# Four blocks of attention and gated MLP: order of the first V pass, of block 1's score sums, and of their store and reload against the weight loads

## The chip, the core and the metric

The kernel runs on one core of one Trainium2 chip. The metric is the device time of one execution in microseconds (us). Executions of the kernel before differ by up to about 1.8 us (1617.65 to 1619.47 us), so effects under 0.5 us are read from the traces, not from the times.

Engine names in the profile: PE is TensorE, PEld its weight load, DVE is VectorE, ACT is ScalarE, POOL is GpSimd, SPq is the queue of SyncE, which issues nearly all DMAs of this kernel in one fixed order.

## The reference, cut to what matters

```python
x = A_x                                            # 2048 tokens x 1024, bf16
x = x + _A_ref(_layernorm(x), A_wqkv, A_wo)        # local dilated attention: 32 heads of 32, 8 keys, step 2
x = x + _B_ref(_layernorm(x), W_gate, W_up, W_down)  # relu(gate) * up, 3584 hidden
x = x + _A_ref(_layernorm(x), A_wqkv, A_wo)
x = x + _B_ref(_layernorm(x), W_gate, W_up, W_down)
```

## The kernel before

Tokens go in blocks of 512 (four tiles of 128). While PE does the gate/up matmuls of block 0, VectorE does the attention of block 1. All steps are "events" with a planned time; sorting the events by that time gives each engine's order of instructions. The planned times set only this order: an instruction runs when its engine reaches it and its data are there. `GRP` (1.73) is the planned time of eight 128x512 matmuls; `t_gu0`, called `at` in the loop, is the planned start of block 0's gate/up matmuls.

The head, the first 11 us (shortened): LayerNorm of block 0, transposed on PE, then V products that start with tile 0 alone.

```python
    def turn(t, halves=(0, 1)):                 # eight transposes; tile 1's in two calls of four
        if t in tps: pass
        elif t == 0: tps[t] = [psum.tile(... tag="acc") for h in range(2)]         # two PSUM tiles
        else:                                                                      # one pair tile
            both = psum_l.tile([P, 2, KC, P], BF16, tag="L", name="tp_pair"); ...
    act_square(2); act_mean(2)                  # ScalarE: tile 2's sums, ahead of the copies
    ...; turn(0); copy(0, "a", ...) x2; ...     # ScalarE copies tile 0's transposes
    def head():
        for kc in range(KC // 2):
            if kc == KC // 2 - 1: ln["second"](0)      # tile 1: first half of the turn, its copy
            for c in range(KC): prod(kc, c, 0, 1)      # V products of tile 0
        ln["second"](1)                                # tile 1: second half
```

Block 1's score sums: sixteen VectorE steps (a product of q and k, an addition), stored to DRAM in two halves, reloaded in another layout, then added over the partitions (`u<-s` in the profile), softmax, weighted V sums (`pv`).

```python
    spread(sums1[:4], t_pv0 + 34.5, 4.5)
    spread(sums1[4:6], t_wo0 + 0.5, 2.5)
    spread(sums1[6:10], t_fill + 1.4, 4.6)
    spread(sums1[10:], t_gu0 + 2.6, 5.4)
    ...
            ev.append((at + 37.5, store_s(1, 1)))        # second half of the sums to DRAM, 0.5 MB
            ev.append((at + 40.5, load_s(1)))            # reload, 4 DMAs, 1 MB in all
            spread(gets2, at + 36.0, 2.5)                # q and k of block 2
            spread(softmax_steps(1), at + 52.0, 3.6)     # starts with u<-s, which waits for the reload
            spread(pv_steps(1), at + 63.0, 5.3)
```

The weights come as 1 MB slabs through a ring of five buffers. A slab load is an event 0.3 after the planned end of the slab whose buffer it takes; an up slab and a gate slab stand at `at + 24 * GRP + 0.3`, that is `at + 41.82`, behind store and reload.

## Time and profile before

| | before |
|---|---|
| time, median of 6 runs | 1618.11 us (1617.65 to 1619.47) |
| span of the profiled run | 1616.4 us |
| PE busy | 1611.3 us |
| PE waits | 1.5 and 0.4 us, both before 9 us |

Two parts of the page of the kernel before: PE's busy time, and the chain of work that ended last.

```profile
PE 1611.3 (100%) x7633; PEld 786.6 (49%) x7633; DVE 1137.1 (70%) x960; ACT 475.8 (29%) x968; POOL 180.4 (11%) x168
PE 99%; DMA 0%; ACT 0%; DVE 0%; issue 0%; ACTq 0%; DVEq 0%
```

The waits of PE in the kernel before (what waited, for whom: us in total, times, longest):

```profile
PE scratch L132 <- DVE ones L310: 1.5, 1, 1.5
PE acc_v L132 <- ACT xnT_first L328: 0.4, 1, 0.4
```

PE is the bound everywhere, and past 9 us it waits for nobody. A change can win only in the head, and can lose anywhere by making a new wait.

The timeline of PE in the head of the kernel before (start and duration in us, engine, line, operation, names, shapes, count, idle before it and what ended it; the last line of each such view is cut off by the end of its window, so its count says nothing):

```profile
6.97 0.72 PE L385 MATMUL tp<-ident,xn_first 128*128 128x128 bf16 x8
8.09 1.50 PE L132 MATMUL acc_v<-xnT_first,w_v 128*128 128x128 bf16 x24 [0.40 <-ACT xnT_first L328]
9.51 0.40 PE L385 MATMUL tp_pair<-ident,xn_first 128*128 128x128 bf16 x4
9.74 0.61 PE L132 MATMUL acc_v<-xnT_first,w_v 128*128 128x128 bf16 x8
10.42 0.38 PE L385 MATMUL tp_pair<-ident,xn_first 128*128 128x128 bf16 x4
10.64 0.55 PE L132 MATMUL acc_v<-xnT_first,w_v 128*128 128x128 bf16 x7
```

The first V product comes 1.12 us after tile 0's first transpose, tile 1's first product (10.64) 3.67 us after it.

The DMA queue of the kernel before around the second store of the sums (same columns; a line is an issue, and its duration is the time to issue, not the transfer):

```profile
230.70 0.34 SPq L121 DMA_DIRECT2D s_d<-s  x1
231.09 0.42 SPq L121 DMA_DIRECT2D k<-k_d  x1
233.90 4.38 SPq L121 DMA_DIRECT2D s<-s_d  x4
238.32 1.46 SPq L121 DMA_DIRECT2D q<-q_d  x1
239.88 0.39 SPq L121 DMA_DIRECT2D w_u<-in_B_W_up_dram  x1
240.32 1.31 SPq L121 DMA_DIRECT2D w_g<-in_B_W_gate_dram  x1
```

The up slab landed at 246.9 and its first matmul started at 247.27: a margin of 0.4 us.

`hT` are the gate products, the VectorE instructions that free PE's accumulators.

### The profile page before, as it was taken

The page shows a single profiled execution, that of the slowest core. Times are in us where ns is not written, and L with a number is a line of the kernel's source. Part 1 is how long each engine was busy: PE and PEld are TensorE (multiplying, and loading weights), DVE is VectorE, ACT ScalarE, POOL GpSimd, SP SyncE. Part 2 cuts the span into 40 slices and gives each one's busy share as a digit, 9 for nine tenths or more (in the row PEclk, how much of TensorE's full clock was granted, in tenths as well). Part 3 has the DMA queues.
Part 4 walks back from the last instruction along what each step waited for, and adds up shares of the span by engine and source line. Part 5 has one row for each costly group of instructions (what it writes and reads, how often), then busy time and mean ns, then how long its engine had stood idle before and what let it go on. Part 6 is the DMA issues. An engine that isn't in the chain of part 4 may idle for free.

```text
span 1616.4 us, 18930 instructions
## 1 busy us (share of the span) xinstructions
PE 1611.3 (100%) x7633; PEld 786.6 (49%) x7633; DVE 1137.1 (70%) x960; ACT 475.8 (29%) x968; POOL 180.4 (11%) x168
## 2 busy tenths in 40 slices
PE   9999999999999999999999999999999999999999
PEld 6646544444444445444454444544445444444444
DVE  5999989996989698929489293893939939311211
ACT  5853312132116313603136031361313311131110
POOL 2400100010003002300053000530005100000000
PEclk9999999999999999999999999999999999999999
DMA  9868868697669766794847947479574794755452
GB/s 306 180 190 238 224 159 262 183 216 204 208 192 217 200 184 212 192 246 146 227 160 201 240 153 230 152 205 252 165 226 155 203 245 157 209 161 177 157 167 68
DMA packets 407448, 317.92 MB, mean 197 GB/s; under 512 B 166464, under 2 KB 387008, under 8 KB 406848
## 3 DMA queue, kind: packets, MB, share of 16 engines
q1 hardware_dynamic: 406784, 316.13, 69.9%
q8 instruction: 59, 0.97, 0.3%
q10 hardware_dynamic: 576, 0.59, 0.1%
q14 instruction: 29, 0.24, 0.0%
HBM read 266.29 MB, written 34.66 MB: 186 GB/s over the span
## 4 chain that ended last, share of the span: by engine, by line
PE 99%; DMA 0%; ACT 0%; DVE 0%; issue 0%; ACTq 0%; DVEq 0%
PE acc_u L132 24%; PE acc_g L132 24%; PE dacc L132 18%; PE acc_v L132 7%; PE acc_wo L132 7%; PE acc_k L132 7%; PE acc_q L132 7%; PE dacc_pair L132 6%; DMA x<-in_A_x_dram 0%; ACT xn_first L328 0%; PE tp_pair L385 0%; PE L L132 0%; DVE x L837 0%; DVE xnT_first L106 0%; ACTq L175 0%
## 5 line engine op out<-in xcount | busy, mean ns | idle before, releaser
L132 PE MATMUL acc_g<-xnT_b,w_g 128*128 128x512 bf16 x1792 | 423.3, 379 | 0.0
L132 PE MATMUL acc_u<-xnT_b,w_u 128*128 128x512 bf16 x1792 | 423.3, 379 | 0.0
L790 ACT ACTIVATE r<-acc_g 128x512 bf16<-128x512 f32 x224 | 133.5, 596 | 726.7 <-PE acc_g L132 701.6
L106 DVE TENSOR_TENSOR hT<-acc_u,r 128x512 bf16<-128x512 f32 x224 | 150.5, 685 | 240.7 <-PE acc_u L132 238.2
L132 PE MATMUL dacc<-w_d,hT 128*128 128x512 bf16 (+1 forms) x1400 | 301.9, 375 | 0.0
L132 PEld LDWEIGHTS <-hT 128*128 128x128 bf16 x1820 | 178.1, 98 | 208.9
L132 PEld LDWEIGHTS <-w_u 128*128 128x128 bf16 x1792 | 175.3, 98 | 211.5
L132 PEld LDWEIGHTS <-w_g 128*128 128x128 bf16 x1792 | 175.4, 98 | 211.4
L106 DVE TENSOR_TENSOR pv<-a,vhm 128x4096 bf16<-128x4096 bf16 x64 | 143.4, 2281 | 0.0
L837 DVE TENSOR_TENSOR x<-dacc,x 128x512 bf16<-128x512 f32 (+1 forms) x38 | 24.5, 672 | 154.2 <-PE dacc L132 154.2
L608 DVE TENSOR_TENSOR t<-q,k 128x2048 f32<-128x2048 bf16 x56 | 128.0, 2292 | 6.7 <-ACT k L543 4.6
L106 DVE TENSOR_TENSOR t<-q,k 128x2048 f32<-128x2048 bf16 x56 | 127.4, 2285 | 3.7 <-ACT k L543 2.6
L106 DVE TENSOR_TENSOR pv<-pv 128x1024 bf16<-128x1024 bf16 (+1 forms) x128 | 113.6, 947 | 0.0
L549 POOL COPY kh<-k 128x14 bf16<-128x14 bf16 x40 | 56.0, 1406 | 504.3 <-ACT k L543 504.3
L132 PE MATMUL acc_wo<-w_o,oT 128*128 128x512 bf16 x512 | 111.8, 379 | 0.0
L621 DVE TENSOR_TENSOR ac<-ac,t 128x2048 f32<-128x2048 f32 x48 | 109.6, 2284 | 0.3
L106 DVE TENSOR_TENSOR ac<-ac,t 128x2048 f32<-128x2048 f32 x48 | 109.5, 2282 | 0.0
L264 POOL TENSOR_TENSOR st_b<-st_b,neg_half 128x1 f32<-128x1 f32 x29 | 43.9, 1523 | 525.8 <-ACT st_b L263 525.7
L132 PE MATMUL dacc_pair<-w_d,hT 128*128 128x512 bf16 x420 | 95.9, 379 | 0.0
L132 PEld LDWEIGHTS <-oT 128*128 128x128 bf16 x512 | 50.0, 98 | 60.4
L259 ACT ACTIVATE xn_b<-x 128x1024 bf16<-128x1024 bf16 x29 | 30.3, 1045 | 129.1 <-DVE x L106 67.0
L446 ACT CAST vT<-acc_v 128x512 bf16<-128x512 f32 x56 | 32.8, 588 | 57.6 <-PE acc_v L132 56.6
(134 smaller groups left out, 1230.0 us busy)
## 6 DMA issues: line engine op xcount, KB each, us to landing
w_g<-in_B_W_gate_dram SPq DMA_DIRECT2D x56, 1024.0 KB, 7.4
w_u<-in_B_W_up_dram SPq DMA_DIRECT2D x56, 1024.0 KB, 5.5
w_d<-in_B_W_down_dram SPq DMA_DIRECT2D x48, 1024.0 KB, 5.7
w_o<-in_A_wo_dram SPq DMA_DIRECT2D x16, 1024.0 KB, 7.0
vhm<-v_d SPq DMA_DIRECT2D x32, 284.0 KB, 6.8
v_d<-vT SPq DMA_DIRECT2D x8, 1024.0 KB, 9.8
oT<-o_d SPq DMA_DIRECT2D x32, 256.0 KB, 4.5
w_d<-in_B_W_down_dram SPq DMA_DIRECT2D x16, 512.0 KB, 3.9
```

What stands on the lines that cost most here:

```text
L106: tail_dve[0] = f(*args, **kwargs).ins
L132: tail_pe[0] = nc.tensor.matmul(*args, **kwargs).ins
L259: nc.scalar.activation(xn, xt[:], ACT.Square, accum_out=sq)
L264: nc.gpsimd.tensor_tensor(rstd, vpe, neg_half[:, 0:1], op=ALU.pow)
L446: tail_act[0] = nc.scalar.copy(st["vT"][:, c, :], acc[:]).ins
L549: nc.gpsimd.tensor_copy(khalo[n][:, c, :], k[:, BLK:BLK + HALO])
L608: nc.vector.tensor_tensor(t[:], i0, i1, op=ALU.mult)
L621: nc.vector.tensor_tensor(o, ac[:], t[:], op=ALU.add)
L790: tail_act[0] = nc.scalar.activation(rs[j][:], acc[:], ACT.Relu).ins
L837: run = dv if n < NB - 2 else (lambda f, *args, **kwargs: f(*args, **kwargs))
```

## The change

Its intent has three parts. Head: do all 32 V products of tile 0 before tile 1's transposes, do these in one go, and move tile 2's mean behind ScalarE's copies, so that the first product comes sooner. Sums: put five of block 1's steps behind LN2 of block 0, so that the gate/up matmuls' input is ready sooner. Store: put store, reload and gets behind the two slab loads, so that a store still waiting for its sums does not hold the weights up.

```diff
-        def turn(t, halves=(0, 1)):
-            if t in tps:
-                pass
-            elif t == 0:
+        def turn(t):
+            if t == 0:
 ...
         act_square(2)
-        act_mean(2)
 ...
         copy(0, "a", 0, KC // 4, KC // 2)
+        act_mean(2)
 ...
-        act_power(2)
 ...
-        def second(h):
-            turn(1, (h,))
-            if h == 0:
-                copy(1, "v", 0)
-                return
+        def second():
+            turn(1)
+            copy(1, "v", 0)
             copy(1, "v", 1)
+            act_power(2)
 ...
             for kc in range(KC // 2):
-                if kc == KC // 2 - 1:
-                    ln["second"](0)
                 for c in range(KC):
                     prod(kc, c, 0, 1)
-            ln["second"](1)
+            ln["second"]()
 ...
-    spread(sums1[4:6], t_wo0 + 0.5, 2.5)
-    spread(sums1[6:10], t_fill + 1.4, 4.6)
+    ev.append((t_wo0 + 0.5, sums1[4]))
+    spread(sums1[5:10], t_fill + 3.3, 3.4)
 ...
-            ev.append((at + 37.5, store_s(1, 1)))
-            ev.append((at + 40.5, load_s(1)))
-            spread(gets2, at + 36.0, 2.5)
+            ev.append((at + 24 * GRP + 0.4, store_s(1, 1)))
+            ev.append((at + 24 * GRP + 0.5, load_s(1)))
+            spread(gets2, at + 24 * GRP + 0.6, 2.5)
```

More of the change, by code (lines that the diff above doesn't have):

```diff
@@ L382, in turn @@
                 tps[t] = [both[:, h, 0:KC // 2, :] for h in range(2)]
-            for c in (h * (KC // 2) + i for h in halves for i in range(KC // 2)):
+            for c in range(KC):
                 with pe_group():
```

## The prediction

> **What bounds the kernel.** TensorE: the busy table gives PE 1611.3 of 1616.4 us, the chain that ended last is 99% PE, the granted clock 1.00. In the waits, PE waited twice: 1.5 us at the start (a memset) and 0.4 us for ScalarE's copy of block 0's first transposes. So only the first 15 us, where PE has holes, or a new hole later can change the time.
>
> **First 11 us, from the timeline (us).** Tile 0's transposes start 6.97. The first V product starts only 8.09: ScalarE's Identity pass for tile 2's mean (1.06, then a 0.19 read) holds its copy until 7.68; copy start to product was 0.41. Products pace at 0.056: 24 reach 9.42, four transposes of tile 1 start 9.51, eight products follow to 10.19. Then PE stands 0.23 us: the other four transposes (10.42) carry a wait on VectorE, whose copy of their sister half ended 10.36. Tile 1's products start 10.64.
>
> The change removes the split and moves the mean behind the copies. The copy then waits for the fourth transpose (ends 7.37), starts near 7.41, products near 7.81: 0.27 gained. All 32 products take 1.78, to 9.60. Tile 1's normalised halves are ready 9.45 and 9.77 as before, so eight transposes run 9.6 to 10.05, the last ending about 10.25. The pair shares one tile, and copies from such a pair start only after the eighth transpose (tile 3: last ends 17.87, copy 17.90). The copy (0.42) then ends near 10.70 and tile 1's products start near 10.75, against 10.64. The early gain becomes a new wait of about 0.5 us for VectorE: net +0.1 us (estimate from these durations, -0.15 to +0.25). Tile 2's variance (0.21), POOL steps (0.19, 0.55) and apply (0.54) end near 12.8; its transposes come at 14.2, so that move is free.
>
> **Block 1's sums.** VectorE's work is only reordered. A step is 4.4 to 4.5 us. LN2 of block 0 should end about 178 instead of 185.8; its last DMA transpose, which landed 189.0 for a first use at 190.29, gets slack. But VectorE will wait for the output projection, so its backlog at gate/up start grows by about 1.3 us: the first gate product moves from 201.46 to 202.7 and ends 203.4; the accumulator that next waits on VectorE starts 204.10. It should just hold; this is the main risk.
>
> **Store and slab.** Before, the second store of sums blocks the queue 11.6 us (queue's waits), so an up-weight slab free at about 230.2 is issued 239.88 and lands 246.9, for use at 247.27. After, it is issued near 230. The reloaded sums arrive 1 to 3 us later; the attention output (stored 297.2, reloaded by 308, used 311.3) still fits. As PE never waited there, nothing is gained.
>
> The Trainium skill ("TensorE: Matmul & The Clock Gate", What's actually happening) says an idle window of about 3.4 us halves the PE clock; here matmuls go from 0.427 to 0.216 us just before the products, and a 0.5 us hole should not undo that.
>
> **Prediction.** 1618.15 us, range 1617.7 to 1618.9. Faster by over 2%: 0.01; within 2%: 0.98; slower: 0.01.
>
> **What would show it.** Timeline: first V product near 7.8; one hole of 0.4 to 0.6 us between tile 1's transposes and products, listed as PE waiting for VectorE's copy; tile 1's products near 10.75; LN2 of block 0 ended near 178; the slab issued 230 to 232; no PE wait after 15 us.
>
> **What would make it wrong.** The copy of tile 1 starting after its fourth transpose (then -0.1 us); PE waiting at 202 to 206 for late gate products (+0.3 to 1.5); later attention output (wait at 311).

## More of the kernel before

Store (230.70), reload (233.90, once the store has landed, 3.2 us after its issue), then the two weight slabs.

VectorE in the kernel before took up the reloaded sums here:

```profile
242.36 0.69 DVE L106 TENSOR_TENSOR hT<-acc_u,r 128x512 bf16<-128x512 f32 x1 [2.76 <-PE acc_u L132]
243.90 2.29 DVE L106 TENSOR_TENSOR u<-s 128x2048 f32<-128x2048 bf16 x1 [0.85 <-DMA s<-s_d]
246.22 1.23 DVE L106 TENSOR_TENSOR u<-u 128x1024 f32<-128x1024 f32 x1
247.37 0.68 DVE L106 TENSOR_TENSOR hT<-acc_u,r 128x512 bf16<-128x512 f32 x1
```

## The result, and the profile after

| | before | after |
|---|---|---|
| time, median of 6 runs | 1618.11 us (1617.65 to 1619.47) | 1621.96 us (1621.52 to 1622.94) |
| span of the profiled run | 1616.4 us | 1620.4 us |
| PE busy | 1611.3 us | 1610.8 us |

The ratio is 1.0023, with a 95% interval of 1.001 to 1.0036: a small loss, 3.85 us by the medians, within 2% but clear of the noise.

The same two parts of the page, for the changed kernel:

```profile
PE 1610.8 (99%) x7633; PEld 786.3 (49%) x7633; DVE 1137.1 (70%) x960; ACT 475.6 (29%) x968; POOL 177.8 (11%) x168
PE 92%; DVE 5%; DMA 1%; issue 1%; SPq 0%; ACT 0%; DVEq 0%
```

The work is the same and the chain is not: 5% of it now runs over VectorE. The waits of PE in the changed kernel say where:

```profile
PE acc_u L132 <- DVE hT L106: 2.2, 2, 1.1
PE scratch L132 <- DVE ones L310: 1.5, 1, 1.5
PE acc_wo L132 <- DVE x L106: 1.0, 1, 1.0
PE tp L383 <- DVE xn_first L106: 0.7, 1, 0.7
PE acc_v L132 <- DMA w_v<-in_A_wqkv_dram: 0.6, 2, 0.3
PE acc_v L132 <- DVE xnT_first L106: 0.5, 1, 0.5
```

Three waits are new and late: two for gate products, one for a residual addition. In the trace they end at 259.2, 274.3 and 318.6 us. Measured as the start-to-start distance of two matmuls less the usual 0.216 they are 1.29, 1.23 and 1.20 us, 3.72 in all. The first matmul of Q starts 0.31 us later than before. Together that is the 4.0 us by which the span grew.

The DMA queue of the changed kernel at the same place:

```profile
230.51 0.37 SPq L121 DMA_DIRECT2D w_u<-in_B_W_up_dram  x1
232.23 0.37 SPq L121 DMA_DIRECT2D w_g<-in_B_W_gate_dram  x1
232.83 0.39 SPq L121 DMA_DIRECT2D s_d<-s  x1
242.22 3.68 SPq L121 DMA_DIRECT2D s<-s_d  x4
```

The slabs go out 9.4 and 8.1 us sooner, as intended. But the store, issued only 2.1 us later than before, has both slabs, 2 MB of weights, in front of it; the first had a start of 2.3 us. The reload, which has to wait for it to land, is issued at 242.22 instead of 233.90: the store took 9.4 us to land instead of 3.2. VectorE in the changed kernel:

```profile
242.67 0.69 DVE L106 TENSOR_TENSOR hT<-acc_u,r 128x512 bf16<-128x512 f32 x1 [2.76 <-PE acc_u L132]
251.35 2.29 DVE L106 TENSOR_TENSOR u<-s 128x2048 f32<-128x2048 bf16 x1 [7.99 <-DMA s<-s_d]
253.67 1.23 DVE L106 TENSOR_TENSOR u<-u 128x1024 f32<-128x1024 f32 x1
254.82 0.68 DVE L106 TENSOR_TENSOR hT<-acc_u,r 128x512 bf16<-128x512 f32 x1
```

VectorE stands 8.0 us for the reload, and the next gate product is done at 255.5 instead of 248.05. The addition comes 7.45 us later: 2.13 from the later issue of the store, 6.19 from its slower landing, less 0.87, because from the issue of the reload to the addition it took 9.13 instead of 10.00 us.

The head of the changed kernel, PE's timeline:

```profile
6.55 0.72 PE L383 MATMUL tp<-ident,xn_first 128*128 128x128 bf16 x8 [0.66 <-DVE xn_first L106]
7.56 1.07 PE L132 MATMUL acc_v<-xnT_first,w_v 128*128 128x128 bf16 x16 [0.28 <-DMA w_v<-in_A_wqkv_dram]
8.92 1.07 PE L132 MATMUL acc_v<-xnT_first,w_v 128*128 128x128 bf16 x16 [0.29 <-DMA w_v<-in_A_wqkv_dram]
9.83 0.61 PE L383 MATMUL tp_pair<-ident,xn_first 128*128 128x128 bf16 x8
10.95 1.22 PE L132 MATMUL acc_v<-xnT_first,w_v 128*128 128x128 bf16 x19 [0.51 <-DVE xnT_first L106]
```

The predicted hole of 0.5 us between tile 1's transposes and its products is there. Two waits for V's first weights also appear in this run. They vary from run to run and are no mark of the new head: a kernel with the old head (e9 below) had two as well, 0.7 us in all. Nor is the wait of 0.7 us before tile 0's transposes: e1 below, with the same head, has none.

### The profile page after: what moved, and what is told of

Same layout as the page of the kernel before. It is cut to its first block, busy times and chain, and to the rows that moved or that the text cites. A ratio compares the mean times of both kernels' runs of the same rounds, so it can differ in the third digit from the quotient of the medians.

```text
span 1620.4 us, 18929 instructions
## 1 busy us (share of the span) xinstructions
PE 1610.8 (99%) x7633; PEld 786.3 (49%) x7633; DVE 1137.1 (70%) x960; ACT 475.6 (29%) x968; POOL 177.8 (11%) x168
## 4 chain that ended last, share of the span: by engine, by line
PE 92%; DVE 5%; DMA 1%; issue 1%; SPq 0%; ACT 0%; DVEq 0%
PE acc_g L132 22%; PE acc_u L132 21%; PE dacc L132 17%; PE acc_k L132 7%; PE acc_q L132 7%; PE acc_v L132 7%; PE acc_wo L132 7%; PE dacc_pair L132 6%; DVE pv L106 2%; DVE ac L106 1%; DVE t L106 1%; DMA s_d<-s 1%; DVE hT L106 0%; DMA s<-s_d 0%; DMA w_v<-in_A_wqkv_dram 0%
```

## The experiments

The theory after reading the result: the loss is the late reload of block 1's sums, behind two slabs, with gate products standing behind it in VectorE's order. The rivals: the reordered sums, which leave VectorE 2 us more backlog; and the head. Eleven kernels were run, all correct, each with five rounds.

Two numbers are read from each trace. **Lateness** is the start of `u<-s` counted from the first gate matmul, less the same in the kernel before (53.61 us). **Loss** is the distance from the first gate matmul to the last matmul of the kernel, less the same in the kernel before (1422.73 us). Start-up jitter is in neither. The distance from the first Q matmul to the first gate matmul was 166.41 us in every trace, so the head and the rest can be read apart.

### e1: the head alone

The kernel before with the head hunks of the diff and no other.

> The kernel before with the head part of the change alone (whole V pass before tile 1's turn, no split of the turn, tile 2's mean behind the copies); sums, store, reload and gets as before. Theory 1 (the late reload of block 1's sums behind two weight slabs makes the loss): within 0.5 us of before, no PE wait after 15 us, tile 1's first product 10.6 to 11.0. Rival (the new head costs most of the 3.9 us): 1.5 us or more above before.

Measured: 1618.23 us median (1617.74 to 1619.77), ratio 1.0002 (0.9989 to 1.0014). Lateness 0.17, loss 0.00. This run had no wait for first weights, so its PE timeline shows the head undisturbed:

```profile
6.52 0.72 PE L383 MATMUL tp<-ident,xn_first 128*128 128x128 bf16 x8
7.38 1.95 PE L132 MATMUL acc_v<-xnT_first,w_v 128*128 128x128 bf16 x32
9.16 0.61 PE L383 MATMUL tp_pair<-ident,xn_first 128*128 128x128 bf16 x8
10.29 0.89 PE L132 MATMUL acc_v<-xnT_first,w_v 128*128 128x128 bf16 x13 [0.52 <-DVE xnT_first L106]
```

The first product comes 0.86 us after the first transpose instead of 1.12, tile 1's first product 3.77 instead of 3.67. What is won at the front is lost at the copy, and 0.1 us more. Tile 1's products came at 10.29, a little under the expected 10.6 to 11.0, because this run's start was 0.45 us early. The head is not the cause of the loss.

### e2: the reordered sums alone

```diff
-    spread(sums1[4:6], t_wo0 + 0.5, 2.5)
-    spread(sums1[6:10], t_fill + 1.4, 4.6)
+    ev.append((t_wo0 + 0.5, sums1[4]))
+    spread(sums1[5:10], t_fill + 3.3, 3.4)
```

> The kernel before with the reordered sums alone (five of block 1's sum steps behind LN2 of block 0); head, store, reload as before. Theory 1: within 0.5 us of before; sums end about 2 us later, store lands about 235.5, slabs issued about 242, so the up slab wanted at 247.3 may come too late: a PE wait of 0 to 2 us for a weight load near 247 is possible. Rival (VectorE's 2 us larger backlog makes the stalls at 259 and 274): at least 2 us above before, PE waits for gate products at 259 and 274.

Measured: 1618.54 us (1618.43 to 1619.34), ratio 1.0003 (0.9991 to 1.0016). Lateness 1.08, loss 0.75. The one late wait of PE in this kernel:

```profile
PE acc_u L132 <- DMA w_u<-in_B_W_up_dram: 0.6, 1, 0.6
```

No gate product is waited for, so the rival of the backlog falls: the reordered sums do not make the loss by themselves, and e3 shows that the loss does not need them. The wait that is there, at 248, is the up slab that had 0.4 us of margin before. So the third part of the change had a reason: with the sums later, a store that blocks the queue makes the weights late.

### e3: store, reload and gets alone

```diff
-            ev.append((at + 37.5, store_s(1, 1)))
-            ev.append((at + 40.5, load_s(1)))
-            spread(gets2, at + 36.0, 2.5)
+            ev.append((at + 24 * GRP + 0.4, store_s(1, 1)))
+            ev.append((at + 24 * GRP + 0.5, load_s(1)))
+            spread(gets2, at + 24 * GRP + 0.6, 2.5)
```

> The kernel before with the store, the reload and the gets of block 1 moved behind the slab loads alone; sums and head as before. Theory 1: 3 to 4.5 us above before; the store of sums takes about 9 us to land instead of 3.2, VectorE waits 6 to 9 us for the reloaded sums, PE waits for gate products near 259 and 274 and for a residual addition near 318. Rival (backlog of the sums or head): within 0.7 us of before.

Measured: 1622.13 us (1620.91 to 1622.27), ratio 1.0022 (1.0009 to 1.0034). Lateness 7.01, loss 3.59, of the changed kernel's 7.14 and 3.71. The late waits of PE are those of the changed kernel:

```profile
PE acc_u L132 <- DVE hT L106: 2.1, 2, 1.1
PE acc_wo L132 <- DVE x L106: 1.0, 1, 1.0
```

This part alone makes the loss.

### e4: the changed kernel with store, reload and gets put back

The diff of e3 reversed, on the changed kernel.

> The changed kernel with the store, the reload and the gets put back where they were (head and sums as changed). Theory 1: 0 to 2 us above before (what is left is the head, 0.3 at most, and a late weight slab near 247 if the sums hold the queue too long); no PE wait at 259 and 274. Rival (sums or head): 3 us or more above before.

Measured: 1619.5 us (1618.98 to 1619.85), ratio 1.0007 (0.9993 to 1.002). Lateness 1.03, loss 0.98, all of it a wait for the up slab near 249; no wait for VectorE after 12 us. By the medians it is 1.4 us above before; in the profiled run the rest is in the head, where PE waited 0.9 us for first weights and the first Q matmul came 0.62 us later than before. As expected, undoing this part brings back most of the loss, and leaves the late slab.

### e5: the softmax later in VectorE's order

On the changed kernel; two more gate products now stand ahead of `u<-s`.

```diff
-            spread(softmax_steps(1), at + 52.0, 3.6)
-            spread(pv_steps(1), at + 63.0, 5.3)
+            spread(softmax_steps(1), at + 60.0, 3.6)
+            spread(pv_steps(1), at + 71.0, 4.8)
```

> The changed kernel with block 1's softmax put 8 us later in the order (and its weighted V sums 8 us later, 4.8 us apart instead of 5.3), so that two more gate products stand ahead of the addition that waits for the reloaded sums; store and reload stay late. Theory (the late reload hurts because gate products stand behind it in VectorE's order): the PE wait near 259 is gone and that near 274 is gone or under 0.5 us; the wait near 318 for the residual addition stays, 0.7 to 2 us; in all 1.0 to 2.5 us above before. Rival (PE stalls for some other reason than this order, for example the backlog of the sums): 3 us or more above before, with waits near 259 as in the changed kernel.

Measured: 1621.27 us (1619.61 to 1622.74), ratio 1.0016 (1.0002 to 1.003). Lateness 6.75, loss 3.81 in the profiled run. The late waits of PE are reduced to this one:

```profile
PE acc_wo L132 <- DVE x L106: 2.0, 1, 2.0
```

The waits at 259 and 274 are gone, as the theory says: they came from gate products standing behind the waiting addition. But the residual addition is as late as before, and its wait, which was 1.20 us, is now 2.12. The expected size (1.0 to 2.5 us) was missed: 3.1 us by the medians, 3.8 in the profiled run. There the hole is only 2.1 us of it; the rest is a slower clock. Two rows from the table of stretches of this kernel (stretch, length, busy us and instructions of PE, PEld, DVE, ACT and POOL, then PE's granted clock, DMA share, GB/s):

```profile
305.00:317.00 12.00, 10.03 (x46) 4.50 (x46) 11.96 (x8) 0.00 (x0) 0.00 (x0) 1.00 1.00 254
318.10:321.40 3.30, 3.30 (x9) 1.21 (x8) 3.30 (x5) 1.36 (x3) 0.00 (x0) 0.51 0.81 254
```

From 1 us after the end of the hole the clock was 0.51 for 3.3 us, then 1.00 again; eight matmuls started 0.427 us apart, and the slow stretch cost 1.7 us against full clock. The mean granted clock is 0.999 in the two longest of the five (1622.25, the profiled one, and 1622.74) and 1.000 in the three others (1619.61 to 1621.27), whose spans are 1.5 to 2.4 us over the 1616.4 of the kernel before. So the wide spread of this kernel's runs goes with a slow clock in some of them, and without it the loss is within the size expected.

### e6: the store on a queue of its own

On the changed kernel, the second store is issued by ScalarE.

```diff
+            if (n, half) == (1, 1):
+                nc.scalar.dma_start(s_d[n % 2][:, ws, :], att[n]["s"][:, ws, :])
+                return
             sp_dma(s_d[n % 2][:, ws, :], att[n]["s"][:, ws, :])
```

> The changed kernel with the second store of block 1's sums issued by ScalarE, so that it has its own DMA queue and does not stand behind the two 1 MB weight slabs in one queue; the order of everything else as changed. Theory (the store lands after 9.4 us because it stands behind 2 MB in its queue): it lands within 4 to 6 us, the addition of the reloaded sums starts 245 to 248.5 instead of 251.3, PE waits near 259, 274 and 318 add up to under 1 us; 0 to 1.3 us above before. Rival (the DMA engines' bandwidth is what the store lacks, whatever its queue): it still takes 8 us or more and the loss stays above 3 us.

Measured: 1619.99 us (1619.75 to 1620.96), ratio 1.0011 (0.9998 to 1.0023). Lateness 5.75, loss 2.32. The store was issued at 232.22 and the reload at 238.90: 6.7 us to land, between the 3.2 with no slab in front and the 9.4 behind two slabs, and above the 4 to 6 expected. The other sizes were missed too: the addition started at 249.34 (245 to 248.5 expected), PE's late waits came to 2.3 us, start to start (under 1 expected), and the medians are 1.8 us apart (0 to 1.3 expected). The rival's sizes (8 us or more to land, a loss above 3 us) did not come either. The Trainium skill ("DMA: Bandwidth & Descriptors", Queues, rings and completion order) says that each DMA engine takes turns between the queues that have work, and (Issuing engines are not separate DMA queues) that the 16 DMA engines are the same whoever issues. The 6.7 us agree with both, and so does the gate slab, which ran beside the store and landed 10.8 us after its issue instead of 8.7: part of the wait was the place in the queue, part the shared engines. Both theories of this experiment hold a share; how large each is was not measured.

### e7: only the store back ahead of the slabs

On the changed kernel: store, two slabs, reload, gets.

```diff
-            ev.append((at + 24 * GRP + 0.4, store_s(1, 1)))
+            ev.append((at + 37.5, store_s(1, 1)))
             ev.append((at + 24 * GRP + 0.5, load_s(1)))
```

> The changed kernel with the second store alone back ahead of the two slab loads in the queue; reload and gets stay behind them. The store waits in the queue for the sums (about 232.5), then lands in 3 to 4 us; the slabs are issued about 233 and land before 243, so no weight wait near 248; the reload is issued about 236 and stands behind 2 MB, the addition starts 244 to 248. Theory: PE waits near 259, 274 and 318 under 0.8 us in all, 0 to 1.2 us above before. Rival (it is the reload behind the slabs, not the store, that costs): addition at 250 or later and 3 us or more above before.

Measured: 1622.95 us (1622.25 to 1623.4), ratio 1.0027 (1.0015 to 1.004): slower than the changed kernel. Lateness 8.63, loss 5.20. Its queue:

```profile
232.24 0.34 SPq L121 DMA_DIRECT2D s_d<-s  x1
232.67 0.39 SPq L121 DMA_DIRECT2D w_u<-in_B_W_up_dram  x1
233.15 0.99 SPq L121 DMA_DIRECT2D w_g<-in_B_W_gate_dram  x1
236.03 10.96 SPq L121 DMA_DIRECT2D s<-s_d  x4
```

The store landed in 3.8 us and the reload was issued at 236.03, 6 us sooner than in the changed kernel. Then the reload took 16.2 us, to the addition at 252.26, instead of 9.1 (10.0 before). The expected gain did not come; the sizes for the rival did. But not the reload alone is at fault, since in the changed kernel the reload had no slab in front and the store had both. The two slabs cost about 6.2 us at either place in the chain of store and reload: it is their 2 MB ahead of the reloaded sums that counts, not the place of the store alone.

### e8: the head with two tiles for tile 1's transposes

On e1: tile 1 gets two PSUM tiles as tile 0 has, so that the first copy need not wait for the eighth transpose.

```diff
-            if t == 0:
-                tps[t] = [psum.tile([P, KC // 2, P], BF16, tag="acc", name=f"tp{h}")[:] for h in range(2)]
+            if t <= 1:
+                tps[t] = [psum.tile([P, KC // 2, P], BF16, tag="acc", name=f"tp{t}{h}")[:] for h in range(2)]
```

> The kernel before with the head of the change, and with tile 1's transposes in two PSUM tiles instead of one pair tile, so that the copy of the first half need not wait for the eighth transpose; the rest as before. If the wait of 0.5 us of PE for VectorE's copy comes from the pair being one tile, it shrinks to 0.2 to 0.35 us: tile 1's first product comes 3.45 to 3.6 us after tile 0's first transpose (3.67 before, 3.77 with the head alone). The time moves by less than the scatter of the runs: within 0.7 us of before.

Measured: 1618.3 us (1617.86 to 1618.81), ratio 0.9999 (0.9987 to 1.0012). Tile 1's first product came 4.24 us after the first transpose, not 3.45 to 3.6, because V's first weights were late in this run. The hole before tile 1's products did shrink as expected (0.2 to 0.35): as the profile counts idle time, from 0.52 us in e1 to 0.29; start to start, less 0.056, from 0.68 to 0.46. In time it is nothing. Lateness 0.61, loss 0.25: at the up slab's first matmul, where e2 and e4 waited too; the profile lists 0.6 us there in which the weight loads waited for this slab.

So the 0.4 us of margin for this slab can run out without the reordered sums.

### e9, e10, e11: one slab instead of two

An order was looked for that keeps the up slab, which has little margin, and the reload in time. The gate slab (used 12 us later) goes behind the reload in all three:

```diff
+            lag = 0.5 if key == ("g", 0, 5) else 0.3
-            events.append((ends[i - RING] + 0.3 if i >= RING else 0.1 * i, ...))
+            events.append((ends[i - RING] + lag if i >= RING else 0.1 * i, ...))
 # e9 (on the kernel before, where the store already stands so) and e10 (on the changed kernel,
 # where the gets already stand so): store, up slab, reload, gate slab, gets
+            ev.append((at + 37.5, store_s(1, 1)))
+            ev.append((at + 24 * GRP + 0.4, load_s(1)))
+            spread(gets2, at + 24 * GRP + 0.6, 2.5)
 # e11 (on the changed kernel, where the gets already stand so): up slab, store, reload, gate slab, gets
+            ev.append((at + 24 * GRP + 0.35, store_s(1, 1)))
+            ev.append((at + 24 * GRP + 0.4, load_s(1)))
+            spread(gets2, at + 24 * GRP + 0.6, 2.5)
```

> The kernel before with the up slab alone issued between the store and the reload of block 1's sums, and the gate slab and the gets behind the reload; head and sums as before. The up slab is issued about 231 and lands before 240, for use at 247.3, so no weight wait is left; the reload stands behind at most 1 MB: the addition of the reloaded sums starts 0.5 to 2.5 us later than before, counted from the first gate matmul. If lateness under 3.43 us is free: from first gate matmul to the end as before within 0.05 us, time within 0.6 us of before. If the tolerance is not real, a PE wait for gate products or residual additions of the size of the lateness.

> The changed kernel with the same order of store, up slab, reload, gate slab, gets. The sums end 2 us later than before, so lateness is 1.5 to 3.3 us. If lateness under 3.43 us is free: no PE wait after 15 us, from first gate matmul to the end within 0.1 us of before, time within 0.8 us of before (the changed head is left). If not: 1.5 us or more above before.

> The changed kernel with only the up slab ahead of the store (half the dose: 1 MB instead of 2 MB), then store, reload, gate slab, gets. The store lands after 5 to 7 us instead of 9.4. Lateness 3.5 to 5.5 us; loss from the first gate matmul on equal to lateness less 3.43, so 0.1 to 2.1 us, and less than the 3.7 of the changed kernel. If the loss is not set by the MB ahead of store and reload, it stays at 3 us or more.

Measured, e9: 1618.02 us (1617.78 to 1618.12), ratio 0.9997 (0.9985 to 1.001); lateness 2.79, a little over the 2.5 expected, loss 0.00. e10: 1619.17 us (1618.21 to 1620.88), ratio 1.0006 (0.9993 to 1.002); lateness 3.40, a little over the 1.5 to 3.3 expected, loss 0.00 in the profiled run. Its lateness is at the edge, and its other runs scatter upwards, by the medians 0.83 us above before (within 0.8 expected); where they lose was not profiled. e11: 1618.2 us (1617.77 to 1618.67), ratio 0.9999 (0.9986 to 1.0011); lateness 1.77, loss 0.00. For e11 a lateness of 3.5 to 5.5 us and a loss of 0.1 to 2.1 us had been expected; the store behind one slab landed in 4.1 us, not 5 to 7. Its queue shows why:

```profile
230.02 0.37 SPq L121 DMA_DIRECT2D w_u<-in_B_W_up_dram  x1
232.34 0.34 SPq L121 DMA_DIRECT2D s_d<-s  x1
236.43 3.59 SPq L121 DMA_DIRECT2D s<-s_d  x4
240.12 1.52 SPq L121 DMA_DIRECT2D w_g<-in_B_W_gate_dram  x1
```

The slab had 2.3 us of transfer behind it before the store, whose sums were not ready sooner, was issued. In the changed kernel the gate slab is issued 0.6 us ahead of the store, so that it stands in front as well.

All traces with a late reload, side by side (computed from the starts of instructions in the traces):

| kernel | lateness us | loss us | late PE waits are for |
|---|---|---|---|
| before | 0 | 0 | none |
| e11 | 1.77 | 0.00 | none |
| e9 | 2.79 | 0.00 | none |
| e10 | 3.40 | 0.00 | none |
| e6 | 5.75 | 2.32 | VectorE |
| e3 | 7.01 | 3.59 | VectorE |
| changed | 7.14 | 3.71 | VectorE |
| e7 | 8.63 | 5.20 | VectorE |

In the last four rows lateness less loss is 3.43, 3.42, 3.43 and 3.43 us. Up to 3.4 us of lateness is free; beyond it each microsecond costs one. (e5 has another order on VectorE and is no part of this row; e2, e4 and e8 lose by the up slab, not by the reload.) The gets, which the change moved along with store and reload, are late in e9, e10 and e11 too, so their place costs nothing by itself.

No version beat the kernel before by more than the scatter. e11 keeps all three aims of the change, the slab in time among them, at no loss that the runs can tell.

## Why the prediction was wrong

It said 1618.15 us, 1617.7 to 1618.9; the time is 1621.96.

- **The step that failed is a term of the sum that was mis-sized**: "The reloaded sums arrive 1 to 3 us later; the attention output ... still fits. As PE never waited there, nothing is gained." They arrived 7.14 us later, counted from the first gate matmul. That they would be later was named; that VectorE would stand 8.0 us for them, with gate products behind, was not. At 1 to 3 us it would have cost nothing: e9 and e11, at 2.79 and 1.77, lost 0.00. What the size lacks is the store's own landing, 9.4 us behind 2 MB instead of 3.2. The prediction does not say how it came to 1 to 3 us; the later issue of the store alone measured 2.13, so the size fits a reckoning that moved the store in the order and left its landing time about as it was.
- **The check was made at the wrong place.** The attention output was set against its first use at 311 us, and there PE did not wait. PE waited sooner, for the gate products behind the waiting addition (259 and 274), and at 318 for a residual addition that frees an accumulator. e5 shows that the first two come from VectorE's order. None of the three cases listed under "What would make it wrong" came.
- **The backlog of the sums, called "the main risk", was none.** e2 shows no wait for a gate product. The first gate product came at 203.59 in the changed kernel (201.46 before, 202.7 predicted), and no wait stands between 202 and 206.
- **Store and slab.** "After, it is issued near 230": 230.51, right. That the early slab wins nothing was right for the kernel before, but not the whole of it: with the sums reordered and the store left in front, the slab comes late and costs 0.75 us (e2) and 0.98 (e4).
- **The head was right.** Net +0.1 us predicted from the first transpose to tile 1's products, +0.10 in e1 (3.77 against 3.67), with the hole of 0.5 us for VectorE's copy. The new head gave 3.76 or 3.77 in e6, e7 and e10 as well; the old one gave 3.56 in e3, so the cost is 0.1 to 0.2 us. The absolute times (7.8 and 10.75) were 7.56 and 10.95, because the start of a run varies (tile 0's transposes start at 6.44 to 7.04 in the thirteen traces) and V's first weights came late.
- **LN2 of block 0** should have ended about 178; its last apply was done at 179.0 (185.9 before).
- **"No PE wait after 15 us"** was wrong, for the reason above.
- The clock window of the Trainium skill ("TensorE: Matmul & The Clock Gate", What's actually happening), cited for the 0.5 us hole: no run shows a slow clock after that hole. In the kernel before, 512-column matmuls start 0.427 us apart up to 6.6 us and 0.216 apart later; between them stand the 128-column ones of the head, 0.056 apart. e5 shows a slow clock after a longer hole, below.

## What to carry to other kernels

All of this was seen in one kernel at one place. A transfer that was moved behind others in a queue came late by what was left of their transfers, not by its place in the order: 6.2 us behind two slabs (the changed kernel), 0.9 us behind one that had a start of 2.3 us (e11). Where a reload has to wait for a store, the delay can sit at either link (the store in the changed kernel, the reload in e7): count the bytes ahead of each. A wait of VectorE held up what stood behind it in its order, so ask not only whether the result is in time for its own user, but what the engine owes others meanwhile. Where slack is unknown, measure it by dose: here four orders gave one line (3.43 us free, then one for one), which also says how much of the two competing loads may go first.

## What the Trainium skill lacked or had wrong

- "TensorE: Matmul & The Clock Gate" (What's actually happening; HAM oscillation) puts the danger at idle gaps of about 3.4 us and calls the window free-running. In e5 a hole of 2.1 us was followed by 3.3 us at a granted clock of 0.51; a hole of 1.95 us in e7 and those of up to 1.3 us in the other kernels were not. It is one trace, and only two of the five executions of e5 show a lower mean clock (0.999), so no limit is derived from it.
- "DMA: Bandwidth & Descriptors" says that a queue's descriptors are consumed in ring order and that queues take turns, but its section on queues gives no size for what that does to a small transfer. Here a 0.5 MB store landed in 3.2 us with no slab in front, 4.1 us behind one 1 MB slab issued 2.3 us earlier, 6.7 us on its own queue beside two slabs and 9.4 us behind them.
- No page that was read says how far VectorE may fall behind before PE stops; it was 3.43 us in this kernel at this place. Which accumulators or buffers make up that figure was not taken apart.
